# An adding DMA forms the second-layer low weights of experts two to eight; the first expert's split is one slice longer

## Chip, cores and metric

One NeuronCore of a Trainium2 chip runs the whole program; nothing is exchanged with other cores. The metric is device time in microseconds, the median of several executions. Profiles come from one further execution with the hardware profiler on. "PE" is TensorE, "PEld" its weight load, "DVE" VectorE, "ACT" ScalarE, "POOL" GpSimd, "SP" SyncE.

## What is computed

Three layers in a row on 3072 tokens of width 512, in float32: windowed attention, a two-layer MLP with leaky ReLU, and a mixture of eight experts in which every expert takes exactly 384 tokens (a greedy assignment by the largest gate value):

```python
def _moe2_ref(x, w_gate, w1, w2):
    logits = x @ w_gate
    order = np.argsort(-logits.flatten())
    for idx in order:
        tok, e = (int(idx) // E, int(idx) % E)
        if assigned[tok] >= 0 or counts[e] >= cap: continue
        assigned[tok] = e; counts[e] += 1
    for e in range(E):
        h = np.maximum(x[assigned == e] @ w1[e], 0.0)
        out[assigned == e] = h @ w2[e]
```

## The kernel before

Float32 products are made of three passes on PE: each operand is split into a high part (the value rounded to the type that PE reads) and a low part (value minus high part), and high*high, low*high and high*low are summed in PSUM.

**The expert stage** (function `phase2`, about 620 to 987 us) handles the experts p = 0 to 7 one after the other, each in eight slices f of the hidden layer. For a slice:

- `load` (L592) brings 128x1024 floats, first-layer weights in columns 0 to 511 and second-layer weights in 512 to 1023, into a `west` buffer (L602; a ring of four; for the first expert two halves in the ring `x`). For each half h, ACT writes the high part (L610) and DVE the low part, raw minus high (L612). A ring buffer is free for the next load when both halves have been read.
- `gemm1` (L618, matmuls L630) makes 12 matmuls into one of two PSUM buffers `ph`; ACT evicts the high part `gh` (L637) and DVE the low part `gl` (L639), which frees the `ph` buffer. With two such buffers, a third slice's gemm1 waits for the first one's `gl`.
- `gemm2` (L646, matmuls L655) adds nine matmuls, three for each of three token tiles.

**The first expert** is special: its third token tile arrives late, so its first FA = 4 slices run gemm1 on 256 columns (tiles 0 and 1) and later again on 128 columns (tile 2, buffers `egb`).

**The routing** of experts 1 to 6 runs beside that on DVE: a search of six steps for each expert, where each step is `below` (DVE, L284/L291 `d` and L301 `cm`), `count` (PE, L318, six or twelve small matmuls), `enough` (DVE, L325 to L336 `fl`) and `base` (PE, L340 `pb`); then `ranks` (PE, L429), `slots`, `places`, `parts` (DVE, L437 to L456), `tokens` (PE, L467), `indices` (DVE, L475 to L479 `idx`), the gather of the token rows (POOL, L482) and, when it lands, transposes (PE, L487), `x1h` (ACT, L490) and `x1l` (DVE, L494). Each expert's result goes out by a scatter from POOL (L673).

**What sets the order.** The program is a list of operations with estimated durations and keys. A planner (class `Plan`) runs through them at build time and writes the instructions of each engine in the order in which it let them start; among operations that are ready on an engine the smallest key goes first. Routing has keys near -1000, weights and gemms of slice s about 200 + s. On the chip each engine runs its list strictly in order, and waits where an operand isn't there.

Of the kernel before, what the change touches and what calls it, by code (L numbers as in the profile page):

```python
# [15 lines left out]
AF = mybir.ActivationFunctionType  # L16
OP = mybir.AluOpType
# [197 lines left out]
def phase2(tc, P, C, ident, L, x2d, we, out, ps_h, ps_o, ps_y, pools, lready, xready, open_pools, open_experts, room, roomy, X0, rows, r_xt, r_g):  # L215
# [9 lines left out]
    KD = DM // 128  # L225
# [5 lines left out]
    HOLD = 2.0  # L231
    LATE, SLACK = 0.5, 0.7
    SW = 0.08
    FA = 4
    V, G, S = nc.vector, nc.gpsimd, nc.scalar
    R = [dict() for _ in range(E)]
    A = {}
# [272 lines left out]
    X, XT = {}, {}  # L510
# [81 lines left out]
    def load(p, f):  # L592
        P.key = 200 + NF * p + f - (6 if p or f < FIRST else 2)
        w = [r.take() for r in r_w[f]]
        n = 2 if p == 0 else 1
        d = []
        for b in [(ps_y if p == 0 else r_west).take() for _ in range(n)]:
            c = slice(1024 // n * len(d), 1024 // n * (len(d) + 1))

            def fn(b=b, c=c):  # L600
                src = we[bass.ds(R[p]["reg"], 1)].rearrange("a p f d -> (a p) f d")
                nc.sync.dma_start(b.t, src[:, f, c])  # L602

            d.append((b, P.dma(2.2 / n, fn, [REG[p]], [b], [open_experts if p else []])))
        o = []
        for h in range(2):
            sl = slice(512 * h, 512 * h + 512)
            b, l = d[h % n]
            raw = lambda b=b, h=h: b.t if n == 2 else b.t[:, 512 * h:512 * h + 512]
            a = P.op(("S", 0.53), lambda sl=sl, raw=raw: S.activation(w[0].t[:, sl], raw(), AF.Copy), [l], [b, w[0]],  # L610
                     () if p else [roomy[f], XT[0][:2] if f >= FIRST else []], late=HOLD if p else 0.0)
            o.append([a, P.op(("V", 0.61), lambda sl=sl, raw=raw: V.tensor_tensor(  # L612
                w[1].t[:, sl], raw(), w[0].t[:, sl].bitcast(FT), op=OP.subtract), [a], [b, *w])])
        W[p, f] = w, o
# [3 lines left out]
    def gemm1(p, f, lo=0, hi=TB):  # L618
        s = NF * p + f
        P.key = 200 + s  # L620
        w, o = W[p, f]
        xs = X[p]
        c, k = slice(lo, hi), hi - lo
        ph = ps_h.take()
        gh, gl = (r.take() for r in (r_gb if lo else r_g))

        def mm(n):
            a, x = ((0, 0), (1, 0), (0, 1))[n // KD]
            d = n % KD
            nc.tensor.matmul(ph.t[:, :k], w[a].t[:, d * 128:(d + 1) * 128], xs[x].t[:, d, c],  # L630
                             start=(n == 0), stop=(n == 3 * KD - 1))

        t = []
        for n in range(3 * KD):
            t = [P.op(("T", {128: 0.112, 256: 0.122, TB: 0.178}[k]), lambda n=n: mm(n),
                      [o[0], XT[p][lo // 128:hi // 128], t], [ph, *w, *xs])]
        a = P.op(("S", 0.42), lambda: S.activation(gh.t[:, :k], ph.t[:, :k], AF.Relu),  # L637
                 [t, [] if p else open_experts], [ph, gh])
        b = P.op(("V", 0.47), lambda: V.scalar_tensor_tensor(  # L639
            gl.t[:, :k], ph.t[:, :k], 0.0, gh.t[:, :k].bitcast(FT), op0=OP.max, op1=OP.subtract), [a], [ph, gh, gl])  # L640
        for i in range(lo // 128, hi // 128):
            GL[s, i] = gh, gl, 128 * i - lo, [a, b]
# [3 lines left out]
    def gemm2(p, f, tiles=range(TT)):  # L646
        s = NF * p + f
        P.key = 200 + s + 2
        w, o = W[p, f]
        if f == 0 and p not in ACC:  # L650
            ACC[p] = [r.take() for r in ps_o]

        def mm(i, n, gh, gl, at):
            l, a = ((gh, 0), (gh, 1), (gl, 0))[n]
            nc.tensor.matmul(ACC[p][i].t, l.t[:, at:at + 128], w[a].t[:, 512:1024],  # L655
                             start=(f == 0 and n == 0), stop=(f == NF - 1 and n == 2))

        for i in tiles:
            gh, gl, at, done = GL.pop((s, i))
            if p == E - 1 and f >= NF - 2:  # L660
                P.key = 200 + NF * p + NF + 1 + i + (f - NF) / 4
            for n in range(3):
                q = PREV[i] = P.op(("T", 0.235), lambda i=i, n=n, gh=gh, gl=gl, at=at: mm(i, n, gh, gl, at), [done[:1 + n // 2], o[1], PREV.get(i)],
                                   [ACC[p][i], gh, gl, *w])
            if f < NF - 1:
                continue
            y = ps_y.take()
            o2 = P.op(("S", 0.53), lambda i=i, y=y: S.activation(y.t, ACC[p][i].t, AF.Copy), [q], [ACC[p][i], y])

            def fn(i=i, y=y):  # L670
                if stores:
                    G.memset(rt([1, 1], FT, "spacer"), 0.0)
                st = G.indirect_dma_start(  # L673
                    out=out, out_offset=bass.IndirectOffsetOnAxis(ap=R[p]["idx"][:, i:i + 1], axis=0),
                    in_=y.t, in_offset=None)
                for other in stores:
                    tc.declare_no_dep(st.ins, other.ins, reason="a token has one expert: rows of other tokens")
                stores.append(st)

            o2 = P.op(("G", 1.04), fn, [o2], [y])  # L680
            P.dep(P.op(("D", 1.05), None, (), [y]), [o2], lat=1.6)


    for p in range(E):
        if p < E - 1:
            search(p)
        else:
            P.key = -1000 + 10 * p
            filled[p] = P.op(("V", 1.0), lambda: last(p), chain, after=[gathered.get(p - 2)])
        number(p)  # L690
        tail(p)
        first = []
        if p == 0:
            for lo, hi in ((0, TB - 128), (TB - 128, TB)):
                tiles = range(lo // 128, hi // 128)
                for f in range(FA + 2):
                    if f < FA:
                        if lo == 0:
                            load(p, f)
                        gemm1(p, f, lo, hi)  # L700
                    if f >= 2:
                        gemm2(p, f - 2, tiles)
            first = range(FA)
        for f in range(NF):
            if f not in first:
                load(p, f)
                gemm1(p, f)
            s = NF * p + f - 2
            if s >= 0 and s not in first:
                gemm2(*divmod(s, NF))  # L710
        if p == E - 1:
            gemm2(p, NF - 2)
            gemm2(p, NF - 1)
# [3 lines left out]
def kernel(ctx, tc, q, k, v, w, w_gate_t, we, out):  # L717
# [515 lines left out]
    def expert_pools():  # L1233
# [7 lines left out]
    rows.view = lambda x: x.rearrange("p a b -> p (a b)").bitcast(FT)  # L1241
    o2 = P.op(("X", 0.0), expert_pools, [[d if t < NTILE - 1 else d.queue for t, d in X2D], list(PREV.values())])
    phase2(tc, P, C, ident, L, x2d, we, out, r_h, r_o, r_x2, pools, ls, X2D, o1, o2,
           [x.rearrange("p a b -> p (a b)") for x in win],
           [[GT[s] for s in range(SL * NF, NJ * NF)] + [[], list(PREV.values())][f >= 3] for f in range(NF // 2)], [r.take() for r in r_x1], rows, r_x1, r_g)
# [57 lines left out]
```

## Time and profile before

| | |
|---|---|
| runs | 986.81, 988.23, 990.12 us; median 988.23 |
| profiled execution | 989.57 us, of which the span of instructions 987.6 us |
| busy | PE 98%, PEld 85%, DVE 78%, ACT 45%, POOL 13% |
| DMA | 95.5 MB, mean 97 GB/s |

How to read it: a busy time is a sum of an engine's instructions; matmuls overlap and their ends are modelled, so the distance from one matmul's start to the next tells more of PE than its busy share. An idle time belongs to the instruction behind it, with the one that ended the wait. The granted TensorE clock stands beside each stretch, 1.00 for 2.4 GHz and 0.50 for 1.2 GHz. The few microseconds between span and execution time lie before the first and after the last instruction.

### The profile page before, as it was taken

The page shows a single profiled execution, that of the slowest core. Times are in us where ns is not written, and L with a number is a line of the kernel's source. Part 1 is how long each engine was busy: PE and PEld are TensorE (multiplying, and loading weights), DVE is VectorE, ACT ScalarE, POOL GpSimd, SP SyncE. Part 2 cuts the span into 40 slices and gives each one's busy share as a digit, 9 for nine tenths or more (in the row PEclk, how much of TensorE's full clock was granted, in tenths as well). Part 3 has the DMA queues.
Part 4 walks back from the last instruction along what each step waited for, and adds up shares of the span by engine and source line. Part 5 has one row for each costly group of instructions (what it writes and reads, how often), then busy time and mean ns, then how long its engine had stood idle before and what let it go on. Part 6 is the DMA issues. An engine that isn't in the chain of part 4 may idle for free.

```text
span 987.6 us, 17321 instructions
## 1 busy us (share of the span) xinstructions
PE 969.7 (98%) x6070; PEld 839.8 (85%) x6070; DVE 771.1 (78%) x2577; ACT 444.0 (45%) x1191; POOL 128.3 (13%) x145
## 2 busy tenths in 40 slices
PE   9999999999999999999999999998999999999997
PEld 7778888888888888888888999777888888888996
DVE  7999798698698689689779984587899998877610
ACT  7777634444444544444554433023424433435511
POOL 0678521000000000000000000010120120220211
PEclk9999999999999999999999999998999999999999
DMA  8656520011111121121120000045452642635500
GB/s 270 219 203 234 187 60 30 30 64 58 30 62 42 47 63 30 56 66 31 49 73 12 1 1 1 33 139 171 129 174 74 223 161 75 235 113 174 184 33 33
DMA packets 36327, 95.50 MB, mean 97 GB/s; under 512 B 4368, under 2 KB 8464, under 8 KB 36112
## 3 DMA queue, kind: packets, MB, share of 16 engines
q1 hardware_dynamic: 32256, 81.54, 25.3%
q0 software_dynamic: 3840, 12.59, 3.8%
q8 instruction: 48, 0.79, 0.3%
q14 instruction: 39, 0.32, 0.1%
q10 hardware_dynamic: 144, 0.26, 0.1%
HBM read 81.79 MB, written 12.58 MB: 96 GB/s over the span
## 4 chain that ended last, share of the span: by engine, by line
PE 83%; DVE 8%; issue 4%; ACT 2%; POOL 1%; DMA 1%; POOLq 0%; DVEq 0%; ACTq 0%; SPq 0%
PE po L1064 24%; PE ph L970 23%; PE ph L630 13%; PE po L655 12%; PE pa L852 3%; DVE junk L1094 2%; PE pa L922 2%; PE pa L895 2%; DVE wp L947 1%; DVE wa L949 1%; DMA wst<-in_w_dram 1%; PE pt L487 1%; DVE wp L946 1%; ACT X L861 1%; PE pc L318 1%
## 5 line engine op out<-in xcount | busy, mean ns | idle before, releaser
L1094 DVE CUSTOM_DVE_ANT_0 junk<-x,wgb 128x512 bf16<-128x512 f32 x296 | 207.6, 701 | 5.4 <-DMA wgb<-in_w_gate_t_dram 1.0
L978 ACT ACTIVATE gs<-ph 128x384 f32<-128x384 f32 x128 | 62.7, 490 | 185.2 <-PE ph L970 181.5
L1064 PE MATMUL po<-wouth,gh 128*128 128x512 f32 x321 | 130.8, 408 | 1.1 <-ACT wouth L953 0.9
L1064 PE MATMUL po<-woutl,gh 128*128 128x512 f32 x321 | 127.7, 398 | 1.7 <-POOL woutl L954 1.7
L979 DVE TENSOR_TENSOR gs<-ph,gs 128x384 f32<-128x384 f32 x128 | 71.1, 556 | 72.4 <-ACT gs L978 71.6
L1064 PE MATMUL po<-wouth,gl 128*128 128x512 f32 x321 | 126.5, 395 | 0.7 <-POOL gl L981 0.6
L861 ACT ACTIVATE X<-X,st 96x128 f32<-96x128 f32 x248 | 96.7, 392 | 47.8 <-DVE st L856 47.6
L970 PE MATMUL ph<-x1h,winh 128*128 128x384 f32 x512 | 111.3, 339 | 0.0
L970 PE MATMUL ph<-x1h,winl 128*128 128x384 f32 x512 | 110.7, 337 | 0.2 <-POOL winl L954 0.2
L970 PE MATMUL ph<-x1l,winh 128*128 128x384 f32 x512 | 109.6, 335 | 0.0
L970 PEld LDWEIGHTS ph<-x1h,winh 128*128 128x128 f32 x512 | 91.7, 188 | 9.2
L637 ACT ACTIVATE gh<-ph 128x384 fp32r<-128x384 f32 (+1 forms) x64 | 31.0, 485 | 142.7 <-PE ph L630 131.1
L970 PEld LDWEIGHTS ph<-x1h,winl 128*128 128x128 f32 x512 | 92.0, 188 | 1.9 <-POOL winl L954 0.8
L970 PEld LDWEIGHTS ph<-x1l,winh 128*128 128x128 f32 x512 | 90.6, 188 | 0.5
L1064 PEld LDWEIGHTS po<-wouth,gh 128*128 128x128 f32 x321 | 60.3, 188 | 14.9 <-ACT wouth L953 1.6
L1064 PEld LDWEIGHTS po<-wouth,gl 128*128 128x128 f32 x321 | 60.2, 188 | 14.9 <-POOL gl L981 2.0
L1064 PEld LDWEIGHTS po<-woutl,gh 128*128 128x128 f32 x321 | 60.3, 188 | 12.9 <-POOL woutl L954 3.0
L639 DVE SCALAR_TENSOR_TENSOR gl<-ph,gh 128x384 fp32r<-128x384 f32 (+1 forms) x64 | 34.9, 546 | 45.8 <-ACT gh L637 44.7
L980 ACT ACTIVATE gh<-gs 128x384 fp32r<-128x384 f32 x107 | 56.1, 524 | 31.9 <-DVE gs L979 31.6
L856 DVE CUSTOM_DVE_ANT_0 X<-pa,masks 96x128 f32<-96x128 f32 x232 | 56.0, 281 | 4.3 <-PE pa L852 4.3
L1180 POOL IOTA ij<- 128x128 int32 x1 | 0.2, 236 | 411.9 <-DVE L L1094 411.9
L981 DVE TENSOR_TENSOR gl<-gs,gh 128x384 fp32r<-128x384 f32 x83 | 45.8, 552 | 9.4 <-ACT gh L980 9.3
(260 smaller groups left out, 1948.0 us busy)
## 6 DMA issues: line engine op xcount, KB each, us to landing
west<-in_we_dram SPq DMA_DIRECT2D x56, 512.0 KB, 4.5
wst<-in_w_dram SPq DMA_DIRECT2D x32, 512.0 KB, 4.8
vt<-in_v_dram SPq DMA_DIRECT2D x30, 256.0 KB, 2.6
kt<-in_k_dram SPq DMA_DIRECT2D x30, 256.0 KB, 3.4
qt<-in_q_dram SPq DMA_DIRECT2D x31, 192.0 KB, 3.2
x2d<-x SPq DMA_DIRECT2D x21, 256.0 KB, 2.2
x<-in_we_dram SPq DMA_DIRECT2D x16, 256.0 KB, 2.8
wgb<-in_w_gate_t_dram SPq DMA_DIRECT2D x1, 2048.0 KB, 7.2
```

The costliest lines, as they stand in the source:

```text
L630: nc.tensor.matmul(ph.t[:, :k], w[a].t[:, d * 128:(d + 1) * 128], xs[x].t[:, d, c], start=(n == 0), stop=(n == 3 * KD - 1))
L639: b = P.op(("V", 0.47), lambda: V.scalar_tensor_tensor(gl.t[:, :k], ph.t[:, :k], 0.0, gh.t[:, :k].bitcast(FT), op0=OP.max, op1=OP.subtract ...
L655: nc.tensor.matmul(ACC[p][i].t, l.t[:, at:at + 128], w[a].t[:, 512:1024], start=(f == 0 and n == 0), stop=(f == NF - 1 and n == 2))
L856: V.tensor_tensor_reduce(out=X.t[:, h, :], in0=ps[h % 2].t[:QB, h // 2 * 128:h // 2 * 128 + 128], in1=masks[:, var, :], scale=-scale, scal ...
L861: S.activation(X.t[:, h, :], X.t[:, h, :], AF.Exp, bias=st.t[:, 0, h:h + 1], scale=-1.0, accum_out=st.t[:, 2, h:h + 1])
L970: nc.tensor.matmul(ph.t[:, :TB], win[wt][:, f, kk * 128:(kk + 1) * 128], xt.t[:, kk, :], start=(n == 0 and kk == 0), stop=(n == 2 and kk = ...
L978: o = P.op(("S", 0.37), lambda: S.activation(t.t, ph.t[:, :TB], AF.Copy, scale=0.01), [o], [ph, t], key=k)
L979: o = P.op(("V", 0.47), lambda: V.tensor_tensor(t.t, ph.t[:, :TB], t.t, op=OP.max), [o], [ph, t], key=k)
L980: x = P.op(("S", 0.42), lambda: S.activation(gh(), t.t, AF.Copy), [o, gd], [t, *gb], key=k)
L981: y = P.op({"V": 0.47} if j > 1 else {"V": 0.47, "G": 0.96} if j else {"G": 0.96}, lambda e=V if j > 1 else G: e.tensor_tensor(gl(), t.t, ...
L1064: nc.tensor.matmul(acc.t, lt()[:, sl], wout[wt][:, f, :], start=(f == 0 and n == 0), stop=(n == 2 and (f == NF - 1 or s == S6 - 1)), skip_ ...
L1094: V.tensor_tensor_reduce(out=pools["wgb"].tile([128, DM], BF, name="junk"), in0=x, in1=WGB[0][:, e, :], scale=1.0, scalar=0.0, op0=OP.mult ...
```

## The change

Three things are edited. (1) For experts 1 to 7 the low part of the second-layer half is no longer a DVE subtraction: ACT writes the negated high part of the raw weights into the low buffer (a second copy with scale -1), and a DMA issued by POOL adds the raw weights onto it, from SBUF to SBUF. The raw buffer is in use until that DMA has landed. There are 7 x 8 = 56 such halves, each 128x512 floats (256 KB). (2) FA goes from 4 to 5: one more slice of the first expert is split. (3) In the planner's list gemm1's first eight matmuls depend only on the high parts of the tokens (`x1h`), and only the last four on the low parts.

```diff
-    FA = 4
+    FA = 5
...
             a = P.op(("S", 0.53), lambda sl=sl, raw=raw: S.activation(w[0].t[:, sl], raw(), AF.Copy), [l], [b, w[0]],
                      () if p else [roomy[f], XT[0][:2] if f >= FIRST else []], late=HOLD if p else 0.0)
+            if p and h:
+                m = P.op(("S", 0.53), lambda sl=sl, raw=raw: S.activation(w[1].t[:, sl], raw(), AF.Copy, scale=-1.0), [l], [b, w[1]], late=HOLD)
+                g = P.op(("G", 1.0), lambda sl=sl, raw=raw: G.dma_start(w[1].t[:, sl], raw(), accum_op=OP.add), [m], [b, w[1]])
+                y = P.op(("D", 2.0), None, (), [b, w[1]])
+                P.dep(y, [g], lat=2.0)
+                o.append([a, y])
+                continue
             o.append([a, P.op(("V", 0.61), lambda sl=sl, raw=raw: V.tensor_tensor(
                 w[1].t[:, sl], raw(), w[0].t[:, sl].bitcast(FT), op=OP.subtract), [a], [b, *w])])
...
-                      [o[0], XT[p][lo // 128:hi // 128], t], [ph, *w, *xs])]
+                      [o[0], [x[:1 + n // (2 * KD)] for x in XT[p][lo // 128:hi // 128]], t], [ph, *w, *xs])]
```

The planner answers with another order on every engine. Line numbers of the changed program are 7 higher from L612 on (L619 for L612, L637 for L630, L646 for L639, L662 for L655).

**Place A, the switch to the first expert's third tile.** PE, from the transposes of that tile on; before:

```order
L487 MATMUL pt<-ident,xg_7580 128x128 x4
L429 LDWEIGHTS ones
L429 MATMUL pt<-F,ones 128x24
L429 LDWEIGHTS tri
L429 MATMUL pt<-F,tri 128x24
L630 MATMUL ph<-x1h,winh 128x128
```

and changed:

```order
L487 MATMUL pt<-ident,xg_7583 128x128 x4
L637 MATMUL ph<-x1h,winh 128x256 x4
L637 MATMUL ph<-x1h,winl 128x256 x4
L637 MATMUL ph<-x1l,winh 128x256
L318 LDWEIGHTS cm_7724
L318 MATMUL pc<-oh,cm_7724 128x32
```

The fifth slice's gemm1 on 256 columns stands where the ranks of the second expert stood. On DVE at the same place, changed:

```order
L273 TENSOR_TENSOR oh<-rev,be 128x192
L646 SCALAR_TENSOR_TENSOR gl<-ph,gh 128x256
L284 SCALAR_TENSOR_TENSOR d<-km,zero 128x48
L301 TENSOR_TENSOR cm_7724<-thr_6540,d 128x768
L494 TENSOR_TENSOR x1l<-pt,x1h 128x4x128
L646 SCALAR_TENSOR_TENSOR gl<-ph,gh 128x256
```

Before, `x1l` stood right behind `oh`; now a `gl` and the first search step of the next expert come first.

**Place B, `tokens` of the second expert.** PE; before, the last `base` ahead of it and what follows:

```order
L340 LDWEIGHTS ones
L340 MATMUL pb<-fl_7768,ones 128x1
L655 MATMUL po_7789<-winh,egbh 128x512
L655 MATMUL po_7789<-winl,egbh 128x512
L655 MATMUL po_7582<-winh,gh 128x512
L655 MATMUL po_7582<-winl,gh 128x512
L467 LDWEIGHTS A
L467 MATMUL pt<-rh,A 128x48
```

and changed, from the last matmul of `tokens` on:

```order
L467 LDWEIGHTS A
L467 MATMUL pt<-rh,A 128x48
L662 MATMUL po_7573<-winl,gh 128x512
L662 MATMUL po_7580<-winh,gh 128x512
L662 MATMUL po_7580<-winl,gh 128x512
L340 LDWEIGHTS ones
L340 MATMUL pb<-fl_7835,ones 128x1
L318 LDWEIGHTS cm_7870
L318 MATMUL pc<-oh,cm_7870 128x32
```

`base` now has the next `count` directly behind it. On DVE, changed, from the `fl` that `base` reads:

```order
L336 TENSOR_SCALAR fl_7835<-am_7833 32x1
L619 TENSOR_TENSOR wl_7850<-west,wh_7837 128x512
L475 TENSOR_SCALAR ix<-pt 32x12
L476 TENSOR_TENSOR ix<-pt,ix 32x12
L477 TENSOR_TENSOR ix<-pt,ix 32x12
L479 TENSOR_TENSOR idx<-pt,ix 32x3 x4
L284 SCALAR_TENSOR_TENSOR d<-km,pb,zero 128x48
L301 TENSOR_TENSOR cm_7870<-thr_6544,d 128x768
L619 TENSOR_TENSOR wl_7875<-west,wh_7866 128x512
L646 SCALAR_TENSOR_TENSOR gl<-ph,gh 128x256
```

The indices and the next `cm` stand between `fl` and the `gl` that frees a `ph` buffer; the `cm` before had been made ahead of the indices.

**Place C, `tokens` of the fourth expert.** PE, from its last matmul on; before:

```order
L467 MATMUL pt<-rh,A 128x48
L630 MATMUL ph<-x1h,winh 128x384 x2
L630 MATMUL ph<-x1h,winl 128x384 x3
L340 LDWEIGHTS ones
L340 MATMUL pb<-fl_8941,ones 128x1
L630 MATMUL ph<-x1h,winl 128x384
L630 MATMUL ph<-x1l,winh 128x384 x4
L655 MATMUL po_8903<-winh,gh 128x512
```

and changed:

```order
L467 MATMUL pt<-rh,A 128x48
L662 MATMUL po_8410<-wl_8363,gh 128x512
L662 MATMUL po_8441<-wh_8320,gh 128x512
L662 MATMUL po_8441<-wl_8363,gh 128x512
L662 MATMUL po_8449<-wh_8320,gh 128x512
L662 MATMUL po_8449<-wl_8363,gh 128x512
L340 LDWEIGHTS ones
L340 MATMUL pb<-fl_8883,ones 128x1
L318 LDWEIGHTS cm_8914
L318 MATMUL pc<-oh,cm_8914 128x32
```

Here too the next `count` directly follows `base`, where five matmuls of gemm1 and four of gemm2 stood between them. Nowhere in the order before are the two neighbours.

## Rows read from the trace of the kernel before

**Rows 1.** The page's first part: busy time, share of the span, instructions.

```profile
PE 969.7 (98%) x6070; PEld 839.8 (85%) x6070; DVE 771.1 (78%) x2577; ACT 444.0 (45%) x1191; POOL 128.3 (13%) x145
```

**Rows 2.** Stretches, about the second and the seventh expert: length; busy PE, PEld, DVE, ACT, POOL; clock, DMA share, GB/s.

```profile
731.00:769.00 38.00, 38.00 (x241) 32.02 (x241) 34.96 (x128) 15.74 (x30) 6.47 (x9) 1.00 0.47 148
...
916.00:951.00 35.00, 35.00 (x183) 31.70 (x182) 15.11 (x25) 14.90 (x29) 5.11 (x8) 1.00 0.34 117
```

**Rows 3.** Waits of PE, 600 us to the end: total, times, longest us.

```profile
PE pt L429 <- DVE x1l L494: 2.1, 1, 2.1
PE ph L630 <- DVE fx L437: 0.9, 1, 0.9
```

**Rows 4.** Timeline at the switch: start us, us, engine, line, operation [idle before].

```profile
681.32 0.60 PE L487 MATMUL pt<-ident,xg 128*128 128x128 f32 x4
...
683.01 0.36 DVE L273 TENSOR_TENSOR oh<-rev,be 128x192 bf16<-128x192 f32 x1
683.29 0.68 DVE L494 TENSOR_TENSOR x1l<-pt,x1h 128x512 fp32r<-128x512 f32 x1
...
684.60 0.42 DVE L639 SCALAR_TENSOR_TENSOR gl<-ph,gh 128x256 fp32r<-128x256 f32 x1
...
685.16 0.30 PE L630 MATMUL ph<-x1h,winh 128*128 128x128 f32 x1 [0.94 <-DVE fx L437]
```

**Rows 5.** Stretches during and behind the switch, columns as in rows 2.

```profile
681.00:686.00 5.00, 1.96 (x21) 1.58 (x20) 4.76 (x22) 2.26 (x4) 0.00 (x0) 1.00 0.83 264
686.00:693.00 7.00, 7.00 (x34) 5.12 (x33) 4.25 (x21) 1.31 (x3) 0.00 (x0) 0.51 0.46 174
```

**Rows 6.** Groups by form, 600 us to the end: count, busy us, mean ns, idle before.

```profile
L612 DVE TENSOR_TENSOR wl<-west,wh 128x512 fp32r<-128x512 f32 x64 | 42.3, 684 | 3.6 <-ACT wh L610 1.6 <-ACT x L668 1.5 <-issue 0.6
...
L610 ACT ACTIVATE wh<-west 128x512 fp32r<-128x512 f32 x64 | 36.7, 623 | 2.1 <-DMA west<-in_we_dram 2.1
L673 POOL DMA_INDIRECT out_dram<-x,idx x24 | 25.1, 1044 | 197.7 <-ACT x L668 194.9 <-issue 2.8
```

**Rows 7.** Timeline of PE: neighbouring groups of four matmuls of 256 and of 128 columns.

```profile
673.40 0.64 PE L630 MATMUL ph<-x1h,winl 128*128 128x256 f32 x4
673.88 0.64 PE L630 MATMUL ph<-x1l,winh 128*128 128x256 f32 x4
...
693.97 0.61 PE L630 MATMUL ph<-x1h,winh 128*128 128x128 f32 x4
...
694.42 0.61 PE L630 MATMUL ph<-x1h,winl 128*128 128x128 f32 x4
```

**Rows 8.** Timeline, `tokens` of the third expert to the next `count`.

```profile
730.31 0.32 PE L467 MATMUL pt<-rh,A 128*128 128x48 f16 x6
...
730.89 0.17 PE L340 MATMUL pb<-fl,ones 32*128 32x1 bf16 x1
...
731.27 0.15 DVE L475 TENSOR_SCALAR ix<-pt 32x12 f32<-32x12 f32 x1
...
731.81 0.86 PE L630 MATMUL ph<-x1h,wl 128*128 128x384 f32 x4
731.85 0.70 DVE L479 TENSOR_TENSOR idx<-pt,ix 32x3 int32<-32x3 f32 x4
...
732.51 0.85 PE L630 MATMUL ph<-x1l,wh 128*128 128x384 f32 x4
...
732.88 0.56 DVE L301 TENSOR_TENSOR cm<-thr,d 128x768 bf16<-128x768 bf16 x1
...
733.21 0.86 PE L655 MATMUL po<-wh,gl 128*128 128x512 f32 x3
...
733.91 0.32 PE L318 MATMUL pc<-oh,cm 128*128 128x32 bf16 x6
```

**Rows 9.** DMA issues: count, KB each, median us from issue to landing.

```profile
west<-in_we_dram SPq DMA_DIRECT2D x56, 512.0 KB, 4.5
...
x2d<-x SPq DMA_DIRECT2D x21, 256.0 KB, 2.2
...
x<-in_we_dram SPq DMA_DIRECT2D x16, 256.0 KB, 2.8
```

## The prediction, made before the changed kernel ran

> **What bounds the kernel now.** I read the busy shares first: PE is busy for 98% of the span, DVE for 78% [rows 1]. Then stretches of about one expert each in the expert stage: PE is busy for all 38 us of one beside the routing and for all 35 us of one near the end, while DVE falls from 35 us of 38 to 15 us of 35 [rows 2]. So PE sets the pace there whether DVE is loaded or not. The view of waits says the same: from 600 us to the end PE waits for another engine just twice, 2.1 and 0.9 us [rows 3], both at the switch to the first expert's third token tile. The timeline there shows the chain: PE starts the transposes at 681.32 and is through at 681.92; DVE is in the next expert's search until 683.37, makes `x1l` until 683.97, and PE's next matmul waits for it, because the small PSUM tile is read until then; then comes the second wait [rows 4]. In these 5 us PE is busy for 1.96 us, and in the 7 us behind them the granted clock is 0.51, the lower level, after which it is whole again [rows 5]. At half speed 7 us do the work of 3.6, so the low clock costs 3.4 us. The switch thus loses 3.0 + 3.4 = 6.4 us, and that is all that can be won in this stage.
>
> **The change part by part.** *The adding DMA.* It takes 56 subtractions off DVE, 56 x 0.684 = 38 us [rows 6]. PE didn't wait for them, so this is worth nothing by itself; its worth lies in what the planner makes of a freer DVE. It adds 56 copies to ACT, 56 x 0.623 = 35 us [rows 6]. ACT had 15.7 us of work in 38 [rows 2] and gets some 5 us more for eight slices, so they fit between evictions; if that cover went, each copy ahead of a `gh` would cost PE at most its own 0.62 us. POOL gets 56 DMAs, of 1.04 us each like the scatters [rows 6], and has time, with 6.5 us of work in 38 [rows 2]. What is queued behind them on POOL is gathers and scatters, which are needed an expert later.
>
> How long such a DMA takes to land no row shows. From below: 256 KB land 2.2 us after their issue from SP, or 2.8 from memory [rows 9], so 3.2 us with POOL's share. From above: it reads two operands, 512 KB, which land in 4.5 us [rows 9], so 5.5 us. I take 5, nearer the upper end, since it moves as much. It is hidden as long as the ring of four keeps up: one expert takes 35 us or 4.4 us a slice [rows 2], four buffers 17.5 us; off that go 4.5 us for the load [rows 9] and 3 x 0.62 = 1.9 us for ACT [rows 6], and 11 us are left. So 0 us, from the lower bound as from the upper one.
>
> The Trainium skill's page "DMA: Bandwidth & Descriptors", section "Anatomy of one DMA — SWDGE (gpsimd) path", gives 2.0 us plus the bytes at 436 GB/s, an estimate of 2.6 us for 256 KB; the rows say 2.2 to 2.8 for transfers of that size, and by either the sum is the same.
>
> *FA = 5.* The fifth slice makes 12 matmuls of 256 and 12 of 128 columns in place of 12 of 384. Four of 256 take 0.48 us, four of 128 take 0.45 [rows 7], four of 384 take 0.70 [rows 8]: 3 x (0.48 + 0.45 - 0.70) = +0.7 us of PE work. This isn't hidden, PE being the bound.
>
> *Place A.* PE now has 1.0 us of the fifth slice's gemm1 behind the transposes. But it needs a free `ph` buffer, so a `gl`, and that stands on DVE behind `oh`: 683.37 + 0.42 = 683.8 [rows 4]. PE starts at about 683.9 and has been idle for 2.0 us; after that it needs x1h alone, and work lasts until `x1l` is there. In place of 3.0 us: -1.0. Bounds: the whole wait goes (-3.0), or a wait of the old size stays behind the `gl` (0).
>
> *Place B.* The new order sends `count` directly after `base`. In the trace of before one such chain can be timed: `idx` takes from 731.27 to 732.55, `d` and `cm` until 733.44 [rows 8], so 1.28 + 0.89 us; PE didn't notice, for between `base` at 730.89 and `count` at 733.91 it had a gemm1 and three matmuls of gemm2 [rows 8]. These are gone. At B DVE has a subtraction (0.68 [rows 6]), `idx`, `d` and `cm` to do from `tokens` on: 2.85 us. PE has `tokens`, three matmuls of gemm2 (0.70 for three [rows 8]) and `base`, about 1.1. Idle: 1.75. Then `gemm1` waits for a `gl` behind another subtraction, 0.68 + 0.42 = 1.1 us after `cm`, while PE has a `count` of 0.32 [rows 8]: 0.8 more. Together +2.6. Bounds: with the subtractions done early 1.2, with DVE late by another `gl` 3.0.
>
> *Place C* is the same with five matmuls as cover and no subtraction between: DVE needs 1.28 + 0.89 after `tokens` and 0.3 to 1.3 us ahead of that (the transit, and the `enough` that is still under way), PE has `tokens`, 5 x 0.23 and `base`, about 1.5. Idle 1.0 to 2.0; I take +1.7, as the `enough` has to end first.
>
> *The rest of the new order* holds, by the same pattern, `gl`s that stand further back than before; 0 to 1.1 us (one subtraction and one `gl`), I take +0.6.
>
> *Clock.* A low clock came behind 3 us of idle PE within 3.3 [rows 4, 5]. After the change A has 2.0 us in one piece and B 2.6 in two. I expect one stretch of low clock still, at B in place of A: 0. Bounds: none left, -3.4; one more, +3.4.
>
> Sum: -1.0 + 0.7 + 2.6 + 1.7 + 0.6 = +4.6 us on the profiled execution's 989.57 (span 987.6 and 2 us around it): 994.2. That execution lies 1.34 us above the median of 988.23, so against the runs I say **992.8 us**, 0.5% slower. A measurement of this kernel can tell 0.3%, 3 us, from no change.
>
> **Rivals.** *Two low clocks:* both A's single piece and B's two drop the clock, or C's does. For it: 2.0 us without a pause come near the 3.0 that did it. Against: the first drop makes PE late, and B's wait shrinks. 992.8 + 3.4 = 996.2.
>
> *The losses cancel:* the low clock behind A delays PE by up to 3.4 us while DVE goes on, so that B's 2.6 us vanish, or the clock doesn't fall at all: 992.8 - 2.6 = 990.2 or 992.8 - 3.4 = 989.4, no change that can be told.
>
> *Faster:* the `gl` at A is made early enough for PE to go on without a gap, and the clock stays up; with 38 us less on DVE the search steps at B and C are done before PE asks. Then -3.0 - 3.4 + 0.7 = -5.7, and 988.23 - 5.7 = 982.5. For it: DVE is the engine all these waits end on, and loses a sixth of its work there (8 x 0.684 of 35 us an expert [rows 2, 6]). Against: at B and C `count` needs a `cm` that needs the `base` just ahead of it, which no free DVE can make early. From waits of less than 2.7 us in B, C and the rest it is faster by over 3 us; half of the way gives 985.
>
> *The adding DMA is late:* from 11 us upwards the ring doesn't keep up; loads come late, ACT stands at its copy in front of a `gh`, and PE with it. At 12.6 us a slice takes 0.4 us longer, over the last three experts' 24 slices +10 us: 1003. For it: these DMAs move 256 KB more per slice over the 16 engines, at a DMA share of 0.47 already [rows 2]. Against: twice the upper bound above. The Trainium skill, same page, section "Issuing engines are not separate DMA queues", says that DMAs of all issuers run on the same 16 engines and interleave, which would make this rival's lateness; the share of 0.47 leaves room.
>
> **How the numbers follow.** Forecast 0.38, two low clocks 0.20, cancelling 0.18, faster 0.14, late DMA 0.10. The forecast alone spans 990 to 995: with A and the clock as taken, the lower bounds of B, C and the rest give +1.9, with A at 0 the upper ones +6.8. The range of 987 to 1000 holds these but the faster case and most of the late DMA. Faster by over 0.3% has the faster case and a little of the bounds, 0.15; within 0.3% the cancelling and a bit of the forecast's lower end, 0.20; slower 0.65.
>
> **What would show it.** Right: L612's successor 56 fewer times on DVE, PE waits of 1 to 2 us for `cm` (or the DVE instruction before) at a `count` directly behind `base`, near 690 us and between 755 and 770, one of about 2 us behind the transposes near 682 for a `gl`, and a clock of about 0.5 for one stretch near 690. Wrong: PE busy throughout B and C, no low clock between 680 and 700; or SP and ACT waiting for the adding DMA, with `west` loads late in the last experts.

## The result, and the profile after

The change is slower: 994.31 us (median of 19 runs, 990.98 to 1004.22) against 989.78 us of the kernel before (19 runs beside it, 986.81 to 992.54), a ratio of 1.0059 with an interval of 1.0044 to 1.0075. The forecast was 992.8 us in a range of 987 to 1000. The runs of the change also lie further apart, and they go with the granted clock: 990.98 us at a mean of 0.996, 994.31 at 0.995, 999.86 at 0.990, 1004.22 at 0.985. A line through all 19 rises by 1.0 us for each 0.001 of clock, and 0.001 of some 990 us is just that. The profiled execution of the change (991.8 us, span 989.7, clock 0.996) is one of its better ones.

Busy times of the change; before stands in [rows 1]:

```profile
PE 968.3 (98%) x6082; PEld 839.5 (85%) x6082; DVE 739.5 (75%) x2522; ACT 472.5 (48%) x1248; POOL 179.5 (18%) x201
```

DVE has lost 32 us, ACT has gained 28 and POOL 51, each some 6 or 7 us less than the 38, 35 and 58 (56 x 1.04) of the working. PE, which sets the end, is as busy as before. Its waits from 600 us to the end, where [rows 3] had two at one place (total, times, longest us):

```profile
PE pc L318 <- DVE cm L301: 2.8, 2, 1.7
PE ph L637 <- DVE gl L646: 2.6, 2, 2.2
PE pb L340 <- DVE fl L336: 1.2, 1, 1.2
```

The timeline of the change shows them one by one, first at the switch (A), then at `tokens` of the second expert (B), then at a `base` of the fourth expert's search, then at `tokens` of the fourth expert (C). Columns: start us, us, engine, line, operation, and the idle time ahead of it with what ended it:

```profile
680.13 0.60 PE L487 MATMUL pt<-ident,xg 128*128 128x128 f32 x4
...
682.17 0.36 DVE L273 TENSOR_TENSOR oh<-rev,be 128x192 bf16<-128x192 f32 x1
682.44 0.42 DVE L646 SCALAR_TENSOR_TENSOR gl<-ph,gh 128x256 fp32r<-128x256 f32 x1
682.91 0.74 PE L637 MATMUL ph<-x1h,winh 128*128 128x256 f32 x4 [2.18 <-DVE gl L646]
...
690.45 0.17 PE L340 MATMUL pb<-fl,ones 32*128 32x1 bf16 x1
690.68 0.70 DVE L479 TENSOR_TENSOR idx<-pt,ix 32x3 int32<-32x3 f32 x4
691.72 0.56 DVE L301 TENSOR_TENSOR cm<-thr,d 128x768 bf16<-128x768 bf16 x1
692.33 0.32 PE L318 MATMUL pc<-oh,cm 128*128 128x32 bf16 x6 [1.71 <-DVE cm L301]
...
733.94 0.16 PE L340 MATMUL pb<-fl,ones 32*128 32x1 bf16 x1 [1.18 <-DVE fl L336]
...
761.46 0.17 PE L340 MATMUL pb<-fl,ones 32*128 32x1 bf16 x1
762.73 0.32 PE L318 MATMUL pc<-oh,cm 128*128 128x32 bf16 x6 [1.09 <-DVE cm L301]
```

At B and C the reader sees the pair that the changed order put side by side: `base`, then at once a `count` whose `cm` DVE can begin only after `base`, behind `idx`. Stretches of the change (length; busy PE, PEld, DVE, ACT, POOL; clock, DMA share, GB/s), to be held against [rows 2, 5]:

```profile
681.00:686.00 5.00, 3.09 (x32) 3.05 (x32) 4.69 (x22) 2.24 (x5) 0.00 (x0) 1.00 0.90 291
688.00:693.00 5.00, 3.29 (x33) 2.40 (x32) 4.59 (x21) 3.27 (x7) 2.06 (x2) 1.00 0.38 81
695.00:699.00 4.00, 4.00 (x23) 3.51 (x24) 3.47 (x14) 1.81 (x4) 3.04 (x4) 0.57 1.00 310
731.00:769.00 38.00, 35.59 (x227) 29.34 (x227) 29.68 (x122) 17.00 (x33) 12.53 (x15) 1.00 0.73 197
```

PE now idles in the 38 us from 731 on, where it had been busy throughout. The low clock has moved from behind A to behind B, and in this execution is half as long: 4 us at 0.57 lose 1.7 us, where before 7 us at 0.51 lost 3.4.

**The account of the two profiled executions.** Waits: 2.18 + 1.71 + 1.18 + 1.09, 0.15 right behind the one at C and 0.44 at 837 us are 6.75 us, against 3.0 before: +3.7. The split's extra matmuls: +0.7. Low clock: -1.7. Together +2.7. From the first `count` (620.1 us here, 621.4 before) to the end the two differ by 3.4, so 0.7 us is spread over the stage and not accounted for; the part ahead of it, the same in both, was 1.3 us shorter by chance, and so the spans differ by 2.1. That other runs of the change are slower still goes with their mean clock; none of them was profiled, so where their clock was low is not known.

### The profile page after: what moved, and what is told of

Its sections match the earlier page's. It is cut to its first block, busy times and chain, and to the rows that moved or that the text cites. A ratio compares the mean times of both kernels' runs of the same rounds, so it can differ in the third digit from the quotient of the medians.

```text
span 989.7 us, 17538 instructions
## 1 busy us (share of the span) xinstructions
PE 968.3 (98%) x6082; PEld 839.5 (85%) x6082; DVE 739.5 (75%) x2522; ACT 472.5 (48%) x1248; POOL 179.5 (18%) x201
## 4 chain that ended last, share of the span: by engine, by line
PE 81%; DVE 11%; issue 3%; ACT 2%; DMA 1%; POOL 1%; DVEq 0%; POOLq 0%; ACTq 0%; SPq 0%
PE po L1071 24%; PE ph L977 23%; PE ph L637 13%; PE po L662 11%; PE pa L859 3%; PE pa L929 2%; PE pa L902 2%; DVE junk L1101 2%; DVE wp L954 1%; DVE wa L956 1%; DMA wst<-in_w_dram 1%; PE pt L487 1%; ACT X L868 1%; DVE wp L953 1%; PE pc L318 1%
## 5 line engine op out<-in xcount | busy, mean ns | idle before, releaser
L646 DVE SCALAR_TENSOR_TENSOR gl<-ph,gh 128x384 fp32r<-128x384 f32 (+1 forms) x64 | 34.8, 544 | 56.8 <-ACT gh L644 52.9
```

The costliest lines, as they stand in the source:

```text
L646: b = P.op(("V", 0.47), lambda: V.scalar_tensor_tensor(gl.t[:, :k], ph.t[:, :k], 0.0, gh.t[:, :k].bitcast(FT), op0=OP.max, op1=OP.subtract ...
```

## Experiments

All twelve, with the ratio to the kernel before run beside them, and the time from the first `count` to the end of the profiled execution. That column leaves out the first 620 us, which are the same in all of them but vary by some 4 us between executions.

| | kernel | median us (runs) | ratio, interval | first `count` to end |
|---|---|---|---|---|
| | before | 988 to 990 | 1 | 366.2 |
| | the change | 994.31 (19) | 1.0059 [1.0044, 1.0075] | 369.6 |
| e1 | adding DMA, old order | 998.44 (4) | 1.0092 [1.0075, 1.0110] | 374.6 |
| e5 | e1, last expert on DVE | 994.67 (11) | 1.0050 [1.0037, 1.0064] | 371.6 |
| e9 | e1, ring of five | 998.23 (6) | 1.0100 [1.0076, 1.0124] | 375.6 |
| e8 | adding DMA alone, planned | 997.00 (6) | 1.0085 [1.0063, 1.0106] | 374.7 |
| e10 | FA = 5 alone | 990.59 (12) | 1.0013 [0.9999, 1.0027] | 366.7 |
| e11 | finer dependency alone | 1000.64 (6) | 1.0112 [1.0089, 1.0134] | 375.9 |
| e2 | FA = 5 and dependency | 1002.89 (5) | 1.0141 [1.0117, 1.0165] | 378.7 |
| e3 | the change, `gl` first | 986.12 (12) | 0.9972 [0.9959, 0.9984] | 362.2 |
| e4 | before, `gl` first | 984.09 (6) | 0.9944 [0.9926, 0.9962] | 360.0 |
| e6 | the change, idle PE filled | 993.31 (6) | 1.0042 [1.0028, 1.0056] | 368.8 |
| e7 | before, filled, too short | 989.53 (11) | 1.0000 [0.9990, 1.0010] | 363.2 |
| e12 | before, filled | 986.98 (12) | 0.9973 [0.9961, 0.9986] | 363.6 |

### The adding DMA by itself, in the old order (e1, e5, e9)

```diff
+            if p and h:
+                v = P.op(("V", 0.61), None, [a], [b, *w])
+                m = P.op(("S", 0.0), lambda sl=sl, raw=raw: S.activation(w[1].t[:, sl], raw(), AF.Copy, scale=-1.0), [l], [b, w[1]], late=HOLD)
+                g = P.op(("G", 0.0), lambda sl=sl, raw=raw: G.dma_start(w[1].t[:, sl], raw(), accum_op=OP.add), [m], [b, w[1]])
+                y = P.op(("X", 0.0), None, [v, g], [b, w[1]])
+                o.append([a, y])
+                continue
```

> The kernel before with the adding DMA alone: ACT writes the negated copy and POOL issues the 56 adding DMAs, but the planner books the subtraction on DVE as if it were still there (nothing is issued for it), so that the matmuls of PE stand word for word in the order before, and FA is 4. My theory (the loss is the order, the adding DMA is hidden and the 56 subtractions were off the path): no change against the kernel before, ratio 0.998 to 1.002, the wait of 2.1 us at the switch stays (DVE sits in the search there, not in a subtraction), and no count waits for a cm. Rival (the adding DMA, the 56 copies on ACT or their traffic cost time by themselves): slower by 3 us or more, ratio 1.003 to 1.006, with waits of PE for ACT, or for the low part of the weights, in the last seven experts.

Measured 1.0092: my theory fell. PE's waits of e1 from 600 us on, and its one long stall in the timeline:

```profile
PE pt L487 <- DVE x1l L494: 6.4, 2, 6.1
PE pt L429 <- DVE x1l L494: 2.1, 1, 2.1
PE ph L637 <- DVE fx L437: 0.9, 1, 0.9
```
```profile
917.20 0.95 POOL L482 DMA_INDIRECT xg<-x2d,idx  x1 [0.30 <-issue]
918.15 1.02 POOL L615 DMA_DIRECT2D wl<-west  x1
...
922.07 0.96 POOL L680 DMA_INDIRECT out_dram<-x,idx  x1 [0.21 <-issue]
923.04 1.88 POOL L615 DMA_DIRECT2D wl<-west  x2
...
925.42 0.33 SPq L602 DMA_DIRECT2D west<-in_we_dram  x1
...
931.49 0.63 ACT L610 ACTIVATE wh<-west 128x512 fp32r<-128x512 f32 x1 [5.20 <-DMA west<-in_we_dram]
932.40 0.59 ACT L490 ACTIVATE x1h<-pt 128x512 fp32r<-128x512 f32 x1
933.97 1.12 PE L487 MATMUL pt<-ident,xg 128*128 128x128 f32 x4 [6.06 <-DVE x1l L494]
```

To be read downwards: three gathers end on POOL at 918.15, an adding DMA follows them, three scatters follow that, and two more adding DMAs wait until 923.04. The first one's ring buffer comes free for the next load at 925.42, 7.3 us after its issue. ACT stands 5.2 us at the `wh` of that load, the `x1h` is behind it, and PE's transposes wait 6.06 us. The waits at the switch, 2.1 and 0.9, are those of [rows 3]. A low clock follows the long wait.

e5 takes the adding DMA away at that place (`if p and h and p < E - 1:`).

> The kernel of the first experiment (adding DMA, order of PE as before), but the last expert's eight low parts are subtracted on DVE again, so 48 adding DMAs are left. The first experiment had one long wait, 6.06 us at 927.57: there three gathers and three scatters stand on POOL among the last expert's adding DMAs, so these come late, their ring buffers come free late, the next load of weights lands late and ACT stands at a wh in front of an x1h. My theory now (the adding DMA costs time at this place alone, and the other 48 are hidden): the wait of 6 us and the low clock behind it go, and the time is that of the kernel before, ratio 0.997 to 1.003. Rival (the copies on ACT, or the traffic, cost a little at each of the 56): 995 to 998 us, most of the loss stays.

Measured 1.0050: the long wait went and four of nine thousandths with it, so that place carried about half. The rest stayed, so my theory of one place fell; the rival's number came nearer, but a little at each of the 56 is not what the trace shows. The trace of e5 shows the same chain at the third expert, in front of another `x1h` (the PE row is the view of waits):

```profile
PE pt L487 <- DVE x1l L494: 1.9, 1, 1.9
```
```profile
749.13 0.63 ACT L610 ACTIVATE winh<-west 128x512 fp32r<-128x512 f32 x1 [3.60 <-DMA west<-in_we_dram]
749.66 0.58 ACT L490 ACTIVATE x1h<-pt 128x512 fp32r<-128x512 f32 x1
```

In e1 PE waited 0.39 us at this place, so the length differs between executions. This wait and the low clock behind it (0.79 over the 8 us from 751) make 3.6 of the 5.4 us that the profiled execution of e5 takes longer than before. The rest lies at the switch, whose wait falls ahead of the first adding DMA (691.6 us): 2.5 us in place of 2.1, and a longer low clock behind it, 0.55 over the 10 us from 686.

e9 is e1 with one more ring buffer (`ring(4,` becomes `ring(5,` for `west`).

> The first experiment (all 56 adding DMAs, the planner books the old subtraction) with a fifth buffer in the ring west; the order of PE is that before but for small shifts between 723 and 908 us. My theory after the first and the fifth experiment (the adding DMA holds a ring buffer until it has landed, behind gathers and scatters on POOL's queue, and the ring of four then runs out): no wait of 1 us or more for x1l behind 700 us, ACT waits less than 3 us for loads of weights, the old wait of 2.1 us at the switch stays, and the time is 988 to 990 us. Rival (the traffic of the adding DMAs slows the loads themselves, or the copies on ACT are late): the waits behind 700 us stay in part, 992 us or more.

Measured 1.0100. The wait at 749 us is gone, as it should be if the ring was short there; that at the last expert is not, and is 7.7 us. But the ring is still the bound there. SyncE, which issues the loads, waits 6.2 us for an adding DMA to land (its waits from 923 to 926 us):

```profile
SPq L602 <- DMA wl<-west: 6.2, 1, 6.2
```

It is the one that POOL issued at 916.76, behind three gathers. At 925.13, 8.4 us after that, the load goes out that lands at 931.84, and ACT's `wh` for it stands in front of the `x1h` that PE waits for. In e1 this was the last expert's fifth load, here it is the seventh: in the order that goes with five buffers more loads come before the transposes, so e9 was no clean test of a longer ring. These stretches at the last expert, of e9 and then of before, show the traffic in the column before the last, the DMA share:

```profile
916.00:926.00 10.00, 10.00 (x54) 9.03 (x53) 1.94 (x3) 5.25 (x11) 8.07 (x11) 1.00 1.05 321
926.00:936.00 10.00, 2.31 (x10) 2.13 (x9) 2.90 (x5) 4.53 (x10) 1.71 (x2) 0.75 0.85 208
```
```profile
916.00:926.00 10.00, 10.00 (x54) 9.02 (x53) 6.36 (x11) 7.03 (x14) 5.11 (x8) 1.00 1.00 340
926.00:936.00 10.00, 10.00 (x56) 9.13 (x55) 6.03 (x11) 5.30 (x10) 0.00 (x0) 1.00 0.18 69
```

Before, the DMA engines are full for 10 us there and then have little to do; with the adding DMAs they are full, or nearly, for 20. But the loads are not slower for it than they were there before: 7.1 and 6.7 us for those issued at 918.59 and 925.13, and 7.1 to 7.4 us for the three that the kernel before issued at 919.17, 920.86 and 922.48 (the median over all of its loads is 4.5 [rows 9]). They go out later. Whether that adding DMA was late for full DMA engines or for the gathers and scatters beside it, no run here tells apart. The Trainium skill's page "DMA: Bandwidth & Descriptors", section "Issuing engines are not separate DMA queues", says that DMAs of all issuers run on the same 16 engines; these rows agree, with a share of 1.00 before and 1.05 with POOL's adding DMAs beside SyncE's loads.

### The parts, with the planner told (e8, e10, e11, e2)

e8 is the change with `FA = 4` and the old dependency.

> The adding DMA alone, with FA = 4 and the old dependency, but the planner knows of it and makes its own order. In that order one count directly follows a base. My theory (waits come from where the planner puts a count or a gl, and not from the DMA): one or two waits of 1 to 2 us for cm or gl at other places than in the change, the old wait at the switch besides, no wait for the loads of weights, and 991 to 998 us. Rival (the DVE time that the adding DMA frees is worth something once the planner knows of it): 985 to 988 us.

Measured 1.0085. PE has four waits besides those at the switch, two of 0.8 and 1.2 us at 760 us and two of 1.2 and 0.8 at 839; none is for loads. A low clock follows each pair (0.79 over the 8 us from 761, 0.81 over the 9 from 839). Told of POOL's time, the planner kept the loads in time, and paid in the order instead.

e10 has `FA = 5` alone (the first hunk of the change's diff), e11 the dependency alone (the last), e2 both, all three without the adding DMA.

> The kernel before with FA = 5 alone: no adding DMA, and gemm1 depends on both parts of the tokens from its first matmul on. In the built order no count directly follows a base, and the ranks stand behind the transposes at the switch as before. My theory (of the second experiment's 14 us most is waits that the finer dependency brings, because it puts the fifth slice's gemm1 and the search of the next expert at the switch): the split costs its 0.7 us of matmuls and some waits of less than 1.5 us, 989 to 992 us. Rival (the split brings them): 997 us or more.

> The kernel before with the finer dependency of gemm1 alone: FA = 4, no adding DMA. One count directly follows a base in the built order. My theory: this is the larger part of the second experiment's loss, waits of 1 to 2 us at a count, a base or a gl behind 680 us, and 994 to 1002 us. Rival (FA = 5 is the larger part, or only both together bring it): 988 to 992 us.

> The change without its adding DMA: FA = 5 and the finer dependency of gemm1, with all subtractions on DVE. My theory (what costs time is the planner's answer to these edits): as slow as the change, 992 to 997 us, with a wait of about 2 us for a gl behind the transposes at the switch and one of 1 to 2 us at a count that directly follows a base (the built order has one such place). Rival (the adding DMA or the copies carry the loss): 988 to 990 us, as before.

FA = 5 alone costs 1.3 thousandths, its interval just reaching no change; the dependency alone costs 11, both together 14. So the finer dependency, which asks for less, is the larger part of what e2 loses. Its worst place in e11 is again a `count` right behind `base`:

```profile
727.15 0.16 PE L340 MATMUL pb<-fl,ones 32*128 32x1 bf16 x1 [0.29 <-DVE fl L336]
729.97 0.32 PE L318 MATMUL pc<-oh,cm 128*128 128x32 bf16 x6 [2.66 <-DVE cm L301]
```

In e2 the waits are 8.7 us in all, and the clock is low for a long stretch behind them:

```profile
PE pc L318 <- DVE cm L301: 3.4, 2, 1.7
PE pb L340 <- DVE fl L336: 3.1, 3, 1.7
PE ph L630 <- DVE gl L639: 2.2, 1, 2.2
```
```profile
690.00:700.00 10.00, 6.54 (x50) 5.36 (x49) 9.19 (x36) 3.25 (x7) 3.48 (x3) 0.74 0.50 173
700.00:710.00 10.00, 10.00 (x53) 9.08 (x54) 4.88 (x16) 2.68 (x7) 0.00 (x0) 0.50 0.35 114
710.00:720.00 10.00, 10.00 (x54) 8.28 (x55) 7.16 (x20) 3.94 (x9) 0.00 (x0) 0.73 0.10 18
```

That is (0.26 + 0.50 + 0.27) x 10 = 10 us lost to the clock. The adding DMA, put on top of e2, gives the change: 1.0141 becomes 1.0059. Seen from the other side, `FA = 5` and the dependency, put on top of e8, take 1.0085 to the same 1.0059. The parts don't add up, since each has an order of its own.

### The order on DVE (e3, e4)

```diff
-            gl.t[:, :k], ph.t[:, :k], 0.0, gh.t[:, :k].bitcast(FT), op0=OP.max, op1=OP.subtract), [a], [ph, gh, gl])
+            gl.t[:, :k], ph.t[:, :k], 0.0, gh.t[:, :k].bitcast(FT), op0=OP.max, op1=OP.subtract), [a], [ph, gh, gl], key=-2000)
```

> The change with one key altered in the planner: gl (the low part of the hidden values on DVE, L646) goes ahead of everything that is ready on DVE, the search included. Nothing is computed otherwise; in the built order no count directly follows a base. My theory (all of the change's waits come from where gl and cm stand on DVE): the waits of 1 us and more at the four places go, no stretch of low clock is left between 600 us and the end, and the time is 982 to 986 us, below both kernels. Rival (DVE has no time for both, whichever goes first): the search is late instead, PE waits for transposes or counts, 990 us or more.

> The same key in the kernel before, with neither the adding DMA nor FA = 5. My theory (the 38 us of DVE that the adding DMA frees were never on the path): the same gain, 982 to 986 us, within 2 us of the change with that key. Rival (only the DVE time that the adding DMA frees makes room for gl ahead of the search): 988 to 992 us, or at least 3 us above the change with that key.

Both beat both kernels; e4, 984.09 us and 0.9944, is the best version of this study. PE waits for no engine from 600 us on in either. In e4, two of the stretches of [rows 2, 5] read:

```profile
681.00:686.00 5.00, 5.00 (x29) 4.23 (x28) 4.76 (x22) 1.44 (x4) 0.00 (x0) 1.00 0.36 85
...
731.00:769.00 38.00, 38.00 (x239) 31.56 (x238) 33.91 (x123) 15.68 (x30) 7.03 (x9) 1.00 0.44 141
```

The switch shows how: six matmuls of gemm2 now stand behind the transposes (in e4 from 684.73 to 686.21 us), where PE had nothing, and cover DVE's search until `x1l` is made (from 685.64). e4 needs neither the adding DMA nor FA = 5; with them (e3) it is 2 us slower. The split's 0.7 us is one part. The last evictions are the other: in e3 the last scatter starts 2.6 us behind the start of the last matmul, in e4 1.3, because in e3 the three token tiles end together. First e3's rows, then e4's:

```profile
975.51 1.96 ACT L675 ACTIVATE x<-po 128x512 f32<-128x512 f32 x3 [2.95 <-PE po L662]
...
976.45 0.39 PE L662 MATMUL po<-wh,gl 128*128 128x512 f32 x1
...
979.05 0.96 POOL L680 DMA_INDIRECT out_dram<-x,idx  x1 [0.21 <-issue]
```
```profile
976.88 0.39 PE L655 MATMUL po<-wh,gl 128*128 128x512 f32 x1
977.31 0.60 ACT L668 ACTIVATE x<-po 128x512 f32<-128x512 f32 x1 [0.76 <-PE po L655]
...
978.18 0.97 POOL L673 DMA_INDIRECT out_dram<-x,idx  x1 [0.30 <-ACT x L668]
```

### Idle PE and the clock (e6, e7, e12)

A helper puts small matmuls of constants into a PSUM buffer that the next `count` overwrites:

```diff
+    def fill_pe(n):
+        if n == 0:
+            return
+        t = pools["ps_r"].tile([128, 32], FT, name="pc")
+        for _ in range(n):
+            nc.tensor.matmul(t, C[0]["ones"], C[0]["ones"][:, :32], start=True, stop=True)
```

> The change with small matmuls that nobody reads put on PE where it stands idle: 36 of 128x32 ahead of the fifth slice's gemm1 (place A), 30 ahead of the count behind tokens of the second expert (B), 18 ahead of the one at C. They are somewhat shorter than the waits and move nothing else. My theory (the waits cost their own 4 to 5 us, and what spreads the runs of the change from 991 to 1004 us is low clock behind idle PE): the granted clock stays whole from 640 us to the end, and the runs lie together at 988 to 991 us. Rival (the low clock has another cause, such as the mean load): runs spread as before with a median near 994 us.

> The kernel before with the same kind of filling at its one gap: 36 matmuls of 128x32 ahead of the ranks of the second expert and 14 ahead of the first gemm1 on the third tile. My theory: the waits stay as long, but the low clock behind them goes, 3.4 us less than the kernel before, 984.5 to 986 us. Rival: the low clock stays, 988 to 990 us.

> The seventh experiment with fills of full length: there 36 small matmuls took 0.9 us, 25 ns each, so that 1.2 us of the wait stayed idle; now 84 stand ahead of the ranks and 36 ahead of the gemm1. My theory (low clock follows idle PE, and a fill has to cover the wait): no run has a low clock behind the switch, 985 to 986.5 us, 3 us less than the kernel before. Rival (matmuls of 32 columns do not hold the clock up, or it falls for another reason): 988 to 990 us again.

In e6 and e7 the fill was too short, because I had sized it at 53 ns a matmul from the six of a `count` in 0.32 us [rows 8]. One takes 25 ns: the row's 0.32 us holds the whole duration of the last one, 0.17 us. The Trainium skill's page "TensorE: Matmul & The Clock Gate", section "Wait — 56ns, not 53.3ns?", says that starts never come closer than about 25 ns, which agrees. In e7, with 1.2 us still idle, the mean clock was 0.998 in two of eleven runs (986.1 and 986.2 us, the latter the profiled one) and 0.994 to 0.996 in the others, and the median did not move. In e12 the fill covers the wait:

```profile
681.38 0.60 PE L497 MATMUL pt<-ident,xg 128*128 128x128 f32 x4
681.81 2.25 PE L316 MATMUL pc<-ones 128*128 128x32 bf16 x84
...
684.13 1.05 PE L316 MATMUL pc<-ones 128*128 128x32 bf16 x36
```
```profile
686.00:693.00 7.00, 7.00 (x58) 5.90 (x58) 6.25 (x31) 3.03 (x8) 1.77 (x2) 1.00 0.58 208
```

PE does useful work no sooner than before, and is 0.27% faster: the stretch that had a clock of 0.51 [rows 5] has 1.00. For the kernel before this shows that its 3 us of idle PE bring the low clock, and that small matmuls hold it up there. For the change the evidence is weaker: e6 left 1.4, 0.9 and 0.5 us idle at A, B and C; its profile has no low clock from 640 us to the last matmul, and its runs spread over 3.6 us instead of 13, but one of them still has a mean clock of 0.992, six runs are few and its median is only 1.7 thousandths lower. A longer fill in the change was not tried.

## Why the prediction was right, and where it was not

- **What bounds.** Right: PE set the end, DVE's 32 us less bought nothing by themselves, and e4, which keeps all subtractions on DVE, gains as much as e3 and more.
- **Place A.** Forecast 2.0 us of idle PE for a `gl`, measured 2.18 for a `gl`; -0.9 in place of -1.0 us.
- **Place B.** The first part was forecast as 1.75 us for `cm` and measured as 1.71. The second, 0.8 us for a `gl`, didn't come: behind that `count` PE went on without a gap. B was sized 0.9 us too large.
- **Place C.** Forecast 1.7, measured 1.09 + 0.15.
- **The rest.** Forecast 0.6 in bounds of 0 to 1.1, measured 1.18 + 0.44 = 1.62, above the upper bound. The larger one is a `base` waiting for `fl` at 732 us, which the prediction had not named. That nearly makes up for what B and C lacked, which is luck: all waits together +3.7 us, forecast +3.9.
- **The split.** +0.7 us: groups of 256 and 128 columns run at the pace of [rows 7] (683.49 to 683.96 and 685.22 to 685.66), and FA = 5 alone cost 1.3 thousandths in e10 with two small waits.
- **Clock.** One stretch at B in place of A was right for the profiled execution, at half the length. What failed is the step "I expect one stretch of low clock still": it took one execution's count for the median's. The runs lie from a mean clock of 0.998 to 0.985. In the profiled execution the low clock was 1.7 us less than before, where 0 was forecast; that, and a part ahead of the first `count` that was 1.3 us shorter by chance, put it 2.4 us below the sum of 994.2 that was made for it.
- **The median.** It came out 1.5 us above the forecast, and that is the base of the sum: the 988.23 us are a median of three runs, and the 19 runs beside the change have 989.78. Against those the change is +4.5 us, forecast +4.6. So close a hit is luck in part: the waits came near in sum alone, and the profiled execution itself is only 2.2 us longer than before; the median run has 2.5 us more, of which its mean clock, 0.995 for 0.996, makes some 1 us and the rest is open.
- **The adding DMA at 0.** Right in the change, where PE waits for no load; wrong in its reason. "It is hidden as long as the ring of four keeps up", until 11 us, was an average over a slice; e1 shows PE stalled for 6 us after an adding DMA of 7.3 us, at a place where it stands among gathers and scatters on POOL. What hides it in the change is the planner, which was told of POOL's time (e8 against e1). SyncE does wait for adding DMAs in the change's last experts too, 8.3 and 6.9 us up to 920 and 928 us, a sign that the prediction had listed for being wrong; but from 840 us on ACT waits for no load, and PE neither. Of the range for its landing, both ends can be held against the 37 of SyncE's waits in the change that an adding DMA's landing ended: it came 3.2 to 7.9 us after the issue on POOL, 4.5 in the middle. So the lower end of 3.2 and the 5 that was taken fit, and the upper end of 5.5 doesn't, with 14 of the 37 above it.
- **The cause in the change.** The prediction laid the loss on the order, rightly: in e3, where `gl`'s key alone is changed, all the waits go, and 7.4 us with them. It could not say which edit made the order, and the experiments name no single one. The dependency alone (e11) and the adding DMA alone with the planner told (e8) each cost more than the whole change, and taking out of the change either the adding DMA (e2) or the other two edits (e8) makes it slower. The adding DMA with `FA = 5` and the old dependency was not run.

Of the rivals, the faster case is what e3 did once `gl` went first, at -2.8 thousandths instead of the change's +5.9; the late DMA is what e1 did, in the old order only. Two low clocks may be what the slower runs had: seven of the 19 lie at 996.75 us or more, with mean clocks of 0.992 to 0.985; none of them was profiled. That the losses cancel was not seen: the profiled execution has its waits at A and at B.

## What to carry to other kernels

Where a planner writes the order, an edit that only loosens a dependency can cost more than one that adds work: look in the new order for a result and its next user side by side on the bound engine, and price that chain; a key on the instruction that frees a buffer may be worth more than the engine time saved. A transfer that replaces an engine's work is to be priced where its queue and the DMA engines are fullest, not at the average of a slice. And idle time of TensorE has two prices, its length and the low clock that may follow; where it can't be removed, small matmuls that nobody reads can save the second; in the kernel before they did so where they covered the wait (e12, mean clocks of 0.996 to 0.999), and in two runs of eleven where they covered 40% of it (e7).

## What the runs showed of the hardware

An adding DMA of 256 KB within SBUF takes much of the DMA engines. The software queue's share of the 16 engines' time goes from the first of these rows (before) to the second (the change):

```profile
q0 software_dynamic: 3840, 12.59, 3.8%
```
```profile
q0 software_dynamic: 11904, 27.27, 12.3%
```

0.085 x 989.7 us over 56 of them is 1.5 us of all 16 engines each. The Trainium skill's page "DMA: Bandwidth & Descriptors", section "Anatomy of one DMA — SWDGE (gpsimd) path", gives bytes at 436 GB/s, an estimate of 0.6 us for 256 KB, and 2.6 us with its fixed part; the landings that ended a wait of SyncE in the change came 3.2 us after the issue at the earliest and 4.5 us in the middle (POOL's own 0.9 us of issuing included), so the page's rule is too low for this kind.

The clock fell behind shorter idle times than the 3 us of the kernel before: behind pieces of 2.2 and 1.7 us with work between them (the change at A and B, 0.57 over 4 us), behind a single one of 1.94 us (e5, 0.79 over 8 us), behind two of 0.8 and 1.2 us (e8 at 760 us, 0.79 over 8 us). I had not expected that it would differ so between executions of one program: the change's mean clock lies between 0.998 and 0.985, and in e6 pieces of 1.4 and 0.9 us brought no low clock in the profiled execution.
